# Prompt-phase attention mixer with a gated MLP: where half of each slot's fill work stands, who copies a fill bank, and the order of the last phase's first chunk

## The chip, the cores and the metric

The kernel runs on one core of one Trainium2 chip. The metric is device time in microseconds (us), the median of three runs. A core has a matrix engine (TensorE, PE in the profile, with its weight loads PEld beside it), VectorE (DVE), ScalarE (ACT), GpSimd (POOL), and SyncE (SP), on whose queue nearly all DMA transfers are issued. Matmul results land in PSUM banks, everything else in SBUF.

## The reference

One sequence of 2048 tokens with 512 features, all in float32. Attention has 32 heads of 16 features and looks back over a window of 256 keys; the MLP goes 512 to 1792 to 512. Cut to what matters:

```python
def layernorm(x):                       # no scale, no shift, eps 1e-5
    return (x - mean(x)) / sqrt(var(x) + eps)

def attention(x, wqkv, wo):             # H = 32, Dh = 16, W = 256
    q, k, v = split(x @ wqkv)
    scores = q @ k.T * Dh ** -0.5
    keep = (0 <= i - j) & (i - j < W)   # causal, sliding window
    p = softmax(where(keep, scores, -1e9))
    return merge_heads(p @ v) @ wo

def mlp(x, w1, b1, w2, b2):
    return gelu_tanh(layernorm(x) @ w1 + b1) @ w2 + b2

xn = layernorm(x)
out = x + attention(xn, wqkv, wo) * silu(mlp(xn, w1, b1, w2, b2))
```

## The kernel before, in words

**Number format.** Most matrix products are made with operands split in two: a high part rounded to TensorE's fp32r format and a low part that holds the rest. A product is then three matmuls (high with high, high with low, low with high; `PASSES`). Making such a pair is called splitting: one engine copies into the high part, another subtracts it from the raw value.

**Three phases.** A short prologue normalizes the first rows. Then a main loop (lines 620 to 642) runs t from -16 to 128; a value of t is called a slot here. Last come four chunks of 512 tokens for the MLP and the output (lines 693 to 783).

**What a slot holds.** Attention is done in 8 groups `n` of 4 heads, each over 16 key blocks of 128, so slots 0 to 127 are one block of one group each. On PE a slot issues, in this order:

1. `prob_block(..., 1)`: the scores of two of the four heads of this block into the only tile of its kind in PSUM, `stb`. ACT takes the exp of it into `pt` (SBUF), and POOL masks the triangles at its edges with `affine_select`. Those are the first scores below.
2. `max_block` for the block that is 12 slots ahead (`LEAD`): the same scores once more with queries as rows, into `xy` and `zo`; DVE merges them with a mask (`copy_predicated`) and takes each query's maximum. Every fourth slot `max_rows` transposes the maxima and sends them by DMA into the query rows, so that the scores come out with the maximum subtracted.
3. `fill_in(t, 0)` and `fill_in(t, 1)`: two helpings of other matmul work, called fills, out of the dictionary `fills`.
4. What `plan` has for this slot: copies, splits and DMAs set by `at(t, function, ...)`.
5. `prob_block(..., 0)`: the second scores, for the other two heads, into the same `stb`, with exp and masks.
6. `pv_step(t - 1)`: probabilities times V for the block before, four small matmuls for each of up to three key blocks, into `zo`; ACT copies the result to `oraw`, and every fourth slot a DMA sends it to `oT_d` in DRAM. V has a column of ones, so the sums of the softmax arrive as a row of the same result.

**The fills.** They are the Q/K projections of the next head groups (`pair_qk`, two pairs for each of the groups 1 to 7), the second half of the V projections (`pair_v`), six tiles of the MLP's hidden layer for the first chunk (`pair_h`, tiles f = 2 to 7, kept in DRAM as `h_d`), and the transposes of the MLP's input. `tandem(t0, t1, one, two)` lays two such jobs over the slots t0 to t1. It works with half matmuls: each step issues one with 64 rows on the upper half of the array and one on the lower half, into two PSUM banks `fb[0]` and `fb[1]`, first with one assignment of halves to banks, then with the other. At the first half of slot t1 both banks are complete and two `finish` functions follow. Each copies its bank out of PSUM. For Q/K, `finish` also sets `high` and `low` for slot t1 + 1 (even chunk) or t1 + 4 (odd chunk): a copy into the high part, a subtraction on POOL for the low part, and six sends by DMA from `sh` and `sl` into the rows of the slot buffer (`qk0` or `qk1`) of the group that is to come. `max_block` of that group reads these rows first.

**What sets the order.** The compute engines run their instructions in the order in which the program lists them (an `Ordered` wrapper keeps it); a scheduler may only place the instructions on SP's DMA queue, which then run one after the other. The pools matter too: raw loads, copies on their way, gelu results, sums, attention rows and residual rows all share five buffers of one pool, `t2`.

**The last phase.** A chunk has 14 tiles f of the hidden layer. Per tile: `hidden(f)`, 12 matmuls; `activate(f)`, gelu on ACT and a split into `gh` and `gl` on DVE; `project(f)`, 12 matmuls with the split W2 into the accumulators `accs`. Tiles are two deep: `hidden(f + 2)` stands behind `project(f - 1)`. In chunk 0 six of the tiles come out of `h_d` as `hr` instead, loaded three times two tiles by DMA. Chunk 0 also fetches and splits what W2 is still missing (`settle("w2", f)`, from `W2_FIRST`), loads Wo (`load_wo`), takes the reciprocal of all softmax sums at once (line 752, on a tile `den` of 128 x 512 loaded at f = 1) and sends it to `rden_d`. From f = 10, `load_o` fetches attention rows and reciprocals, and one step later `split_o` multiplies them on POOL and splits them on DVE into `ohl`. After the 14 tiles come silu, the Wo matmuls out of `ohl`, the product with the gate, the sum with x and the store. Input for the next chunk is loaded and normalized in between.

The main loop in its own words:

```python
prob_block(t // 16, t % 16, 1)
max_block(m // 16, m % 16)
fill_in(t, 0)
fill_in(t, 1)
for fn, args in plan.get(t, []):
    fn(*args)
prob_block(t // 16, t % 16, 0)
pv_step((t - 1) // 16, (t - 1) % 16)
```

Of the kernel before, what the change touches and what calls it, by code (L numbers as in the profile page):

```python
# [49 lines left out]
def mixer_kernel(ctx, tc, x, wqk, wv, wo, w1, b1, w2, b2, out):  # L50
# [245 lines left out]
    def pair_qk(n, c):  # L296
# [11 lines left out]
        def finish(ps, t):  # L308
# [3 lines left out]
            nc.scalar.copy(raw, ps)  # L312
# [17 lines left out]
    def pair_v(i):  # L330
# [7 lines left out]
        def finish(ps, t):  # L338
            nc.scalar.copy(vt[:, 2 * i: 2 * i + 2, :, 0:DH], ps.rearrange("p (b h d) -> p b h d", b=2, d=DH))
        return 6 * KT, mm, finish  # L340

    def pair_h(f):
# [5 lines left out]
        def finish(ps, t):  # L348
            raw = t2.tile([P, 512], F32, tag="t2", name=f"hr_{f}")
            nc.scalar.copy(raw, ps)  # L350
            nc.sync.dma_start(h_d[f - 2], raw)
        return 3 * KT, mm, finish

    def tandem(t0, t1, one, two, mid=None, back=None):
# [15 lines left out]
        fills[t1, 0].append((one[2], (fb[0], t1)))  # L370
        fills[t1, 0].append((two[2], (fb[1], t1)))
# [207 lines left out]
    for n, spans in enumerate((((-2, 2), (3, 8)), ((9, 15), (16, 23)), ((24, 31), (32, 39)), ((40, 46), (47, 51)),  # L579
                               ((56, 59), (68, 71)), ((76, 79), (80, 85)), ((86, 91), (92, 97))), 1):  # L580
        for c, (t0, t1) in zip((0, 2), spans):
            tandem(t0, t1, pair_qk(n, c), pair_qk(n, c + 1))
    for i, (t0, t1) in enumerate(((52, 55), (60, 63), (64, 67), (72, 75))):
        tandem(t0, t1, pair_v(2 * i), pair_v(2 * i + 1))
    for f, *at_ in ((2, 106, 112, None, None), (4, 113, 119, 115, None), (6, 120, 127, 123, 125)):
        tandem(*at_[:2], pair_h(f), pair_h(f + 1), *at_[2:])

    for n, t in enumerate((-7, 6, 21, 37, 53, 73, 83), 1):
# [6 lines left out]
    W2_FIRST = 4  # L595
    at(77, open_y)
    for i, t in enumerate((79, 81, 84, 87, 90, 92, 94, 96, 97, 98)):
        at(t, y_steps, i, i + 1)
    at(99, open_w1)
    for k, f in enumerate([*range(2, EARLY + 2), 0, 1, *range(EARLY + 2, NF)]):  # L600
        at(100 + 3 * k // 2, fetch, "w1", f)
        at(102 + 3 * k // 2, settle, "w1", f, k < 6)
    at(113, open_w2, 0)
    for f in range(W2_FIRST):
        at(115 + 3 * f, fetch, "w2", f)
        at(119 + 3 * f, settle, "w2", f)
    for kt in range(KT):
        (_, mm, _), = job_y(kt)[0]
        fills[101 + kt, 1] = [(mm, (0,))]
# [10 lines left out]
    for t in range(-16, end + 1):  # L620
# [13 lines left out]
        fill_in(t, 1)  # L634
        for fn, args in plan.get(t, []):
            fn(*args)
        if 0 <= t < end:
            prob_block(t // 16, t % 16, 0)
        if t >= 1:
# [33 lines left out]
    def fetch_sums():  # L673
        den = t2.tile([P, 512], F32, tag="t2", name="den")
        for g in range(4):
            nc.sync.dma_start(den[32 * g: 32 * g + 32], oT_d[g, :, DH].rearrange("a (c t) -> a c t", c=NCH))
        return den
# [15 lines left out]
    for c in range(NCH):  # L693
# [17 lines left out]

        def project(f):
# [104 lines left out]
```

## Time and profile before

| what | value |
|---|---|
| median of 3 runs | 842.91 us (840.06, 845.07, 842.91) |
| profiled execution, own time | 841.03 us |
| span of the profiled execution | 839.3 us |
| mean granted clock of TensorE | 0.983 |
| HBM read, written | 35.13 MB, 15.99 MB |

```profile
## 2 busy tenths in 40 slices
PE   5998788999989899898889889969999999999997
DVE  6875567877765555868774167342445335442233
ACT  5623567777665564776868622221112211131111
POOL 4002555756554454675755300121011201120013
PEclk9999899999999999999999989979999999999999
```

Each digit stands for a fortieth of the span, 21 us, and gives an engine's busy share in tenths. The loop with its slots fills the slices from the fourth to the twenty-third; the last phase is the rest, in which ACT, DVE and POOL have much less to do. The last row is the clock that TensorE was granted, in tenths of full speed. Span and the run's own time differ by what lies ahead of the first and behind the last instruction.

### The profile page before, as it was taken

How to read it: one execution, taken by the hardware profiler on the slowest of the kernel's cores; microseconds unless marked ns; L12 is line 12 of the kernel's file. 1: busy time of each engine (PE TensorE's matmuls, PEld its weight loads, DVE VectorE, ACT ScalarE, POOL GpSimd, SP SyncE). 2: the span in 40 equal slices, each digit the busy share in tenths (PEclk: the TensorE clock that was granted, in tenths of full speed). 3: DMA queues.
4: the chain of work that ended last, by engine and by line, in shares of the span. 5: the costliest groups of instructions: out<-in, count | busy, mean ns of one | idle time of the engine just before them, and what ended most of it. 6: DMA issues, size and time to landing. Idle time of an engine off the chain costs nothing. (4 is left out here: it accounts for less than half of the span.)

```text
span 839.3 us, 18438 instructions
## 1 busy us (share of the span) xinstructions
PE 760.6 (91%) x7384; PEld 594.0 (71%) x7384; DVE 467.6 (56%) x739; ACT 378.3 (45%) x643; POOL 288.3 (34%) x575
## 2 busy tenths in 40 slices
PE   5998788999989899898889889969999999999997
PEld 4876466666677777665666568748888888888886
DVE  6875567877765555868774167342445335442233
ACT  5623567777665564776868622221112211131111
POOL 4002555756554454675755300121011201120013
PEclk9999899999999999999999989979999999999999
DMA  8442345443453224446525353341013201310023
GB/s 278 149 92 54 91 96 143 103 106 84 118 116 84 68 55 128 96 112 155 138 73 160 102 186 93 107 127 38 12 38 101 101 0 38 92 72 1 26 69 107
DMA packets 51477, 79.98 MB, mean 95 GB/s; under 512 B 10112, under 2 KB 14208, under 8 KB 51392
## 3 DMA queue, kind: packets, MB, share of 16 engines
q1 hardware_dynamic: 51392, 78.80, 33.9%
q8 instruction: 58, 0.95, 0.5%
q14 instruction: 27, 0.22, 0.1%
HBM read 35.13 MB, written 15.99 MB: 61 GB/s over the span
## 5 line engine op out<-in xcount | busy, mean ns | idle before, releaser
L42 POOL TENSOR_SCALAR_AFFINE_SELECT pt<-pt 128x256 f32<-128x256 f32 x480 | 187.3, 414 | 204.8 <-ACT pt L42 202.2
L42 ACT ACTIVATE pt<-stb 128x768 f32<-128x768 f32 (+1 forms) x244 | 189.1, 775 | 112.4 <-PE stb L42 106.6
L42 DVE TENSOR_REDUCE mt<-xy 128x4 f32<-128x1024 f32 (+1 forms) x128 | 152.6, 1193 | 4.4
L42 PE MATMUL acc<-w,gh 128*128 128x512 f32 x448 | 141.5, 396 | 6.3 <-DVE gh L42 3.7
L42 DVE COPY_PREDICATED xy<-upper,zo 128x512 f32<-128x512 int32 x112 | 77.8, 695 | 104.5 <-PE zo L42 102.6
L42 PE MATMUL h<-yh,w1s 128*128 128x512 f32 x400 | 130.3, 389 | 0.4 <-ACT oraw L42 0.4
L42 PE MATMUL stb<-qk 64*128 64x384 f32 (+1 forms) x488 | 95.7, 386 | 35.9 <-ACT pt L42 26.6
L42 ACT ACTIVATE g<-h,b1s 128x512 f32<-128x512 f32 x50 | 34.5, 690 | 185.9 <-PE h L42 182.5
L42 PE MATMUL fb<-xnT,wqb 64*128 64x512 f32 (+1 forms) x720 | 112.7, 412 | 1.1 <-DVE xnT L42 1.1
L42 DVE CAST gh<-g 128x512 fp32r<-128x512 f32 x56 | 26.9, 480 | 152.1 <-PE acc L42 131.3
L42 PE MATMUL zo<-pt,vt 128*17 128x128 f32 x2880 | 104.8, 277 | 2.6 <-DVE xy L42 1.7
L42 PEld LDWEIGHTS acc<-w,gh 128*128 128x128 f32 x448 | 85.5, 191 | 26.6 <-DVE w L42 3.4
L42 PEld LDWEIGHTS stb<-qk 64*128 64x128 f32 x488 | 46.6, 185 | 81.0 <-ACT pt L42 75.1
L42 PEld LDWEIGHTS zo<-pt,vt 128*17 128x17 f32 x2880 | 68.2, 97 | 35.3 <-DVE xy L42 17.6
L42 PE MATMUL acc<-w,gl 128*128 128x512 f32 x224 | 88.5, 395 | 0.0
L42 PEld LDWEIGHTS h<-yh,w1s 128*128 128x128 f32 x400 | 75.1, 188 | 16.2 <-ACT oraw L42 0.7
L42 PE MATMUL h<-w1s 128*128 128x512 f32 x200 | 77.8, 389 | 0.0
L42 PEld LDWEIGHTS fb<-xnT,wqb 64*128 64x128 f32 (+1 forms) x720 | 69.9, 191 | 10.9 <-DVE xnT L42 1.5
L42 PE MATMUL xy<-qk 64*128 64x256 f32 (+2 forms) x536 | 61.9, 304 | 10.1 <-DMA qk<-sl 6.7
L42 POOL TENSOR_TENSOR or<-or,rec 128x512 f32<-128x512 f32 x16 | 21.1, 1318 | 143.6 <-DMA rec<-rden_d 127.5
L42 PEld LDWEIGHTS xy<-qk 64*128 64x128 f32 x536 | 45.3, 186 | 21.2 <-issue 9.1
L42 PE MATMUL s<-wos,ohl 128*128 128x512 f32 x192 | 47.3, 403 | 4.9 <-DVE ohl L42 4.9
(89 smaller groups left out, 848.2 us busy)
## 6 DMA issues: line engine op xcount, KB each, us to landing
qk<-sh SPq DMA_DIRECT2D x128, 128.0 KB
qk<-sl SPq DMA_DIRECT2D x64, 128.0 KB
oT_d<-oraw SPq DMA_DIRECT2D x32, 256.0 KB
x<-in_x_dram SPq DMA_DIRECT2D x16, 256.0 KB
or<-oT_d SPq DMA_DIRECT2D x16, 256.0 KB
rec<-rden_d SPq DMA_DIRECT2D x16, 256.0 KB
xo<-in_x_dram SPq DMA_DIRECT2D x16, 256.0 KB
out_dram<-xo SPq DMA_DIRECT2D x16, 256.0 KB
```

The lines of the kernel that those rows point to most:

```text
L42: r = issue(*args, **kwargs)
```

## The change

The diff does these things:

- In the loop, `fill_in(t, 1)` now stands behind the plan and the second scores, ahead of `pv_step`. `fill_in(t, 0)` stays.
- At the end of a pair, `fb[0]` is still copied by ACT, `fb[1]` by DVE.
- The first two Q/K projections of group 1 are no longer a tandem over slots -2 to 2 that ends with both copies in slot 2. They are two single jobs, spread over the half slots of -2 to 2, each of which sends its rows when it is done. The third and fourth are a tandem over slots 3 to 7 instead of 3 to 8.
- All other spans get new places: Q/K of groups 2 to 7 one to seven slots earlier, the V projections in 54 to 61 and 66 to 73, hidden tiles in 103 to 127 without slots between the pairs. The weights' fetches and splits, the steps that normalize the MLP's input, its transposes and the loads of W1 are set earlier with them.
- `W2_FIRST` goes from 4 to 7: seven W2 tiles are fetched and split in the loop, and `settle` in chunk 0 starts with the eighth, one at each step from the first on.
- `den` is loaded ahead of the chunks. The reciprocal comes in four parts of 128 columns at steps 4 to 7, and is sent at step 7.
- Chunk 0 takes the tiles in the order 2 to 7, 0, 1, 8 to 13, with `hidden(0)` and `hidden(1)` still issued first.
- `load_wo` stays at steps 8 to 11; `load_o` and `split_o` come two steps sooner in all chunks (8 to 11 and 9 to 12); in chunk 0 the loading and normalizing of the next chunk's input starts four steps later.

```diff
--- before.py
+++ after.py
@@ -305,11 +305,11 @@
         def send(src, qk, tt):
             copy_rows(slots[n % 2][tt:P:4, qk, :, sl], src[64 * qk: 64 * qk + 64])
 
-        def finish(ps, t):
+        def finish(ps, t, copy):
             hi = sgp.tile([P, 512], F32R, tag="sh", name=f"sh_{n}_{c}")
             lo = sgp.tile([P, 512], F32R, tag="sl", name=f"sl_{n}_{c}")
             raw = t2.tile([P, 512], F32, tag="t2", name=f"pjr_{n}_{c}")
-            nc.scalar.copy(raw, ps)
+            copy(raw, ps)
 
             def high():
                 nc.scalar.copy(hi, raw)
@@ -335,8 +335,8 @@
             nc.tensor.matmul(ps[:, 256 * j: 256 * (j + 1)], big[r, a, kt, P * kb: P * (kb + 1)], wva[r, b, kt],
                              **flags)
 
-        def finish(ps, t):
-            nc.scalar.copy(vt[:, 2 * i: 2 * i + 2, :, 0:DH], ps.rearrange("p (b h d) -> p b h d", b=2, d=DH))
+        def finish(ps, t, copy):
+            copy(vt[:, 2 * i: 2 * i + 2, :, 0:DH], ps.rearrange("p (b h d) -> p b h d", b=2, d=DH))
         return 6 * KT, mm, finish
 
     def pair_h(f):
@@ -345,9 +345,9 @@
             kt, (a, b) = k // 3, PASSES[k % 3]
             nc.tensor.matmul(ps, mlp["w1"][r, a, f, P * kt: P * (kt + 1)], mlp["yy"][b][kt][r], **flags)
 
-        def finish(ps, t):
+        def finish(ps, t, copy):
             raw = t2.tile([P, 512], F32, tag="t2", name=f"hr_{f}")
-            nc.scalar.copy(raw, ps)
+            copy(raw, ps)
             nc.sync.dma_start(h_d[f - 2], raw)
         return 3 * KT, mm, finish
 
@@ -367,8 +367,8 @@
                     (two if phase == 0 else one)[1](fb[1 - phase], i, hi, **flags)
                     (one if phase == 0 else two)[1](fb[phase], i, lo, **flags)
                 fills.setdefault(places[i * len(places) // n], []).append((unit, ()))
-        fills[t1, 0].append((one[2], (fb[0], t1)))
-        fills[t1, 0].append((two[2], (fb[1], t1)))
+        fills[t1, 0].append((one[2], (fb[0], t1, nc.scalar.copy)))
+        fills[t1, 0].append((two[2], (fb[1], t1, nc.vector.tensor_copy)))
 
     def spread(jobs, places):
 
@@ -576,37 +576,40 @@
     for t0, n, jobs in groups:
         fills.update(spread(jobs, [(t0 + i // 2, i % 2) for i in range(2 * n)]))
 
-    for n, spans in enumerate((((-2, 2), (3, 8)), ((9, 15), (16, 23)), ((24, 31), (32, 39)), ((40, 46), (47, 51)),
-                               ((56, 59), (68, 71)), ((76, 79), (80, 85)), ((86, 91), (92, 97))), 1):
+    for place, todo in spread([job_qk(1, 0), job_qk(1, 1)], [(t, k) for t in range(-2, 3) for k in range(2)]).items():
+        fills.setdefault(place, []).extend(todo)
+    tandem(3, 7, pair_qk(1, 2), pair_qk(1, 3), 6)
+    for n, spans in enumerate((((8, 13), (14, 20)), ((21, 28), (29, 36)), ((37, 42), (43, 48)), ((49, 53), (62, 65)),
+                               ((74, 77), (78, 82)), ((83, 88), (89, 94))), 2):
         for c, (t0, t1) in zip((0, 2), spans):
             tandem(t0, t1, pair_qk(n, c), pair_qk(n, c + 1))
-    for i, (t0, t1) in enumerate(((52, 55), (60, 63), (64, 67), (72, 75))):
-        tandem(t0, t1, pair_v(2 * i), pair_v(2 * i + 1))
-    for f, *at_ in ((2, 106, 112, None, None), (4, 113, 119, 115, None), (6, 120, 127, 123, 125)):
+    for i, (t0, t1) in enumerate(((54, 57), (58, 61), (66, 69), (70, 73))):
+        tandem(t0, t1, pair_v(2 * i), pair_v(2 * i + 1), 67 if t0 == 66 else None)
+    for f, *at_ in ((2, 103, 110, None, None), (4, 111, 118, 114, None), (6, 119, 127, 122, 123)):
         tandem(*at_[:2], pair_h(f), pair_h(f + 1), *at_[2:])
 
-    for n, t in enumerate((-7, 6, 21, 37, 53, 73, 83), 1):
+    for n, t in enumerate((-9, 6, 18, 34, 46, 70, 80), 1):
         at(t - 4, fetch_wqk, n)
         at(t, split_wqk, 0)
         at(t, split_wqk, 1)
     at(20, fetch_wv, 1)
     at(22, split_wv_part, 0)
     at(26, split_wv_part, 1)
-    W2_FIRST = 4
+    W2_FIRST = 7
     at(77, open_y)
-    for i, t in enumerate((79, 81, 84, 87, 90, 92, 94, 96, 97, 98)):
+    for i, t in enumerate((78, 79, 81, 83, 85, 87, 89, 91, 93, 94)):
         at(t, y_steps, i, i + 1)
-    at(99, open_w1)
+    at(95, open_w1)
     for k, f in enumerate([*range(2, EARLY + 2), 0, 1, *range(EARLY + 2, NF)]):
-        at(100 + 3 * k // 2, fetch, "w1", f)
-        at(102 + 3 * k // 2, settle, "w1", f, k < 6)
+        at(96 + 3 * k // 2, fetch, "w1", f)
+        at(98 + 3 * k // 2, settle, "w1", f, k < 6)
     at(113, open_w2, 0)
     for f in range(W2_FIRST):
-        at(115 + 3 * f, fetch, "w2", f)
-        at(119 + 3 * f, settle, "w2", f)
+        at(114 + 2 * f, fetch, "w2", f)
+        at(116 + 2 * f, settle, "w2", f)
     for kt in range(KT):
         (_, mm, _), = job_y(kt)[0]
-        fills[101 + kt, 1] = [(mm, (0,))]
+        fills[98 + kt, 1] = [(mm, (0,))]
 
     ln3 = layernorm(xs[3], "A3", True)
     lns = {-16: ln1[8:] + ln2[5:6], -14: ln2[6:8], -13: ln2[8:] + ln3[0:5], -12: ln3[5:8], -11: ln3[8:]}
@@ -631,11 +634,11 @@
         if 0 <= m < end:
             max_block(m // 16, m % 16)
         fill_in(t, 0)
-        fill_in(t, 1)
         for fn, args in plan.get(t, []):
             fn(*args)
         if 0 <= t < end:
             prob_block(t // 16, t % 16, 0)
+        fill_in(t, 1)
         if t >= 1:
             pv_step((t - 1) // 16, (t - 1) % 16)
         run(lns.get(t, ()))
@@ -670,11 +673,9 @@
         raw = load(t2, "t2", wo[:, 512 * g: 512 * (g + 1)], f"wor{g}")
         split(wos[:, 0, g], wos[:, 1, g], raw)
 
-    def fetch_sums():
-        den = t2.tile([P, 512], F32, tag="t2", name="den")
-        for g in range(4):
-            nc.sync.dma_start(den[32 * g: 32 * g + 32], oT_d[g, :, DH].rearrange("a (c t) -> a c t", c=NCH))
-        return den
+    den = t2.tile([P, 512], F32, tag="t2", name="den")
+    for g in range(4):
+        nc.sync.dma_start(den[32 * g: 32 * g + 32], oT_d[g, :, DH].rearrange("a (c t) -> a c t", c=NCH))
 
     def load_o(c, g):
 
@@ -709,52 +710,53 @@
             split(gh, gl, g, nc.vector.tensor_copy)
             gs[f] = (gh, gl)
 
+        order = [*made, *(f for f in range(NF) if f not in made)]
+
         def project(f):
             gh, gl = gs.pop(f)
             for i in range(4):
                 acc = accs[i // 2][:, i % 2]
                 sl = slice(P * i, P * (i + 1))
                 for k, (a, b) in enumerate(((gh, 0), (gh, 1), (gl, 0))):
-                    nc.tensor.matmul(acc, a[:, sl], w2_part(b, f), start=(f == 0 and k == 0),
-                                     stop=(f == NF - 1 and k == 2))
+                    nc.tensor.matmul(acc, a[:, sl], w2_part(b, f), start=(f == order[0] and k == 0),
+                                     stop=(f == order[-1] and k == 2))
 
         hidden(0)
         hidden(1)
-        for f in range(NF + 1):
-            if f < NF:
-                activate(f)
-            if c == 0 and f < NF:
-                if f >= W2_FIRST:
-                    settle("w2", f)
-                    if f + 2 < NF:
-                        fetch("w2", f + 2)
-                if f >= 8 and f < 12:
-                    load_wo(f - 8)
-            if f >= 1:
-                project(f - 1)
-            if f + 2 < NF and f + 2 not in made:
-                hidden(f + 2)
+        late = 4 if c == 0 else 0
+        for i in range(NF + 1):
+            if i < NF:
+                activate(order[i])
+            if c == 0 and W2_FIRST + i < NF:
+                settle("w2", W2_FIRST + i)
+                if W2_FIRST + i + 2 < NF:
+                    fetch("w2", W2_FIRST + i + 2)
+            if i >= 1:
+                project(order[i - 1])
+            if i + 2 < NF and order[i + 2] not in made and order[i + 2] > 1:
+                hidden(order[i + 2])
+            if c == 0 and 4 <= i < 8:
+                nc.vector.reciprocal(den[:, P * (i - 4): P * (i - 3)], den[:, P * (i - 4): P * (i - 3)])
+                if i == 7:
+                    nc.sync.dma_start(rden_d.rearrange("g a (c t) -> (g a c) t", c=NCH), den)
+            if c == 0 and 8 <= i < 12:
+                load_wo(i - 8)
             if c + 1 < NCH:
-                if f == 2:
+                if i == 2 + late:
                     mlp["y"] = load_x(c + 1, ((mlp["yp"], "y"),), "y")
                     mlp["ln"] = layernorm(mlp["y"], f"C{c + 1}_0", False)
-                elif f == 7:
+                elif i == 7 + late:
                     mlp["ln"] = layernorm(mlp["y"], f"C{c + 1}_1", False)
-                if f in (4, 7):
+                if i - late in (4, 7):
                     y_steps(0, 2)
-                elif f in (5, 8):
+                elif i - late in (5, 8):
                     y_steps(2, 5)
-                elif f in (6, 9):
+                elif i - late in (6, 9):
                     y_steps(5, 10)
-            if c == 0 and f == 1:
-                den = fetch_sums()
-            if c == 0 and f == 4:
-                nc.vector.reciprocal(den, den)
-                nc.sync.dma_start(rden_d.rearrange("g a (c t) -> (g a c) t", c=NCH), den)
-            if 11 <= f < 15:
-                os_.append(split_o(c, f - 11, *wanted))
-            if 10 <= f < 14:
-                wanted = load_o(c, f - 10)
+            if 9 <= i < 13:
+                os_.append(split_o(c, i - 9, *wanted))
+            if 8 <= i < 12:
+                wanted = load_o(c, i - 8)
         us = [accs[i // 2][:, i % 2] for i in range(4)]
         for u in us:
             nc.vector.tensor_add(u, u, b2s)
```

## The prediction, made before the changed kernel had run

> **What bounds the kernel now.** I read the page, busy time by stretch, the waits, the timeline of two slots, then the last phase by itself.
>
> ```profile
> span 839.3 us, 18438 instructions
> PE 760.6 (91%) x7384; PEld 594.0 (71%) x7384; DVE 467.6 (56%) x739; ACT 378.3 (45%) x643; POOL 288.3 (34%) x575
> L42 ACT COPY oraw<-zo 128x128 f32<-128x128 f32 x128 | 34.6, 271 | 5.1 <-PE zo L42 4.9
> ```
>
> TensorE (PE) is the engine to save on. Each slot ends with one copy of the PV result (`oraw`, 128 of them); I used these as slot marks and cut the loop at them (15, 33, 31, 19, 16 and 13 slots), and the last phase at its first two chunks. Columns: length, busy time and instructions of each engine, granted clock, DMA.
>
> ```profile
> 78.50:132.10 53.60, 43.00 (x634) 30.96 (x634) 32.64 (x43) 32.68 (x58) 27.44 (x61) 0.94 0.37 92
> 132.10:227.50 95.40, 87.69 (x1328) 62.22 (x1328) 71.55 (x95) 68.64 (x121) 59.67 (x133) 1.00 0.46 109
> 227.50:339.60 112.10, 100.54 (x1618) 80.17 (x1618) 65.30 (x91) 67.63 (x120) 54.01 (x124) 0.98 0.36 87
> 339.60:396.90 57.30, 51.23 (x764) 36.73 (x764) 43.97 (x63) 40.32 (x71) 36.98 (x80) 1.00 0.52 125
> 396.90:447.30 50.40, 43.25 (x646) 30.75 (x646) 38.21 (x53) 36.54 (x67) 31.57 (x67) 1.00 0.43 123
> 447.30:474.00 26.70, 24.60 (x418) 16.43 (x418) 7.09 (x12) 25.12 (x51) 17.58 (x46) 1.00 0.41 123
> 474.00:569.00 95.00, 80.99 (x328) 63.92 (x329) 48.74 (x88) 25.27 (x39) 11.09 (x9) 0.91 0.41 125
> 569.00:658.00 89.00, 89.00 (x402) 73.78 (x402) 38.52 (x74) 15.16 (x23) 12.59 (x10) 1.00 0.18 60
> ```
>
> The first stretch takes 3.57 us a slot, the second 2.89, the dense third 3.62, the next two 3.02 and 3.15. In chunk 1 of the last phase (569 to 658) PE never rests; chunk 0 is longer, although six of its fourteen hidden tiles were made in the loop. In the loop PE waits for almost one thing, scores behind the exp that empties `stb`:
>
> ```profile
> PEld stb L42 <- ACT pt L42: 75.1, 141, 1.7
> ```
>
> The end of a fill pair, and the slot after it:
>
> ```profile
> 303.21 1.14 PE L42 MATMUL fb<-xnT,wqb 64*128 64x512 f32 x8
> ...
> 304.18 0.33 PE L42 MATMUL stb<-qk 64*128 64x384 f32 x2
> ...
> 304.38 1.07 ACT L42 COPY pjr<-fb 128x512 f32<-128x512 f32 x2 [0.49 <-PE fb L42]
> ...
> 305.34 0.83 ACT L42 ACTIVATE pt<-stb 128x768 f32<-128x768 f32 x1
> ...
> 306.22 0.19 PEld L42 LDWEIGHTS stb<-qk 64*128 64x128 f32 x2 [1.20 <-ACT pt L42]
> ...
> 306.79 0.81 ACT L42 ACTIVATE pt<-stb 128x768 f32<-128x768 f32 x1 [0.46 <-PE stb L42]
> ...
> 307.05 1.68 PE L42 MATMUL fb<-wva,xnT 64*128 64x256 f32 x24
> ...
> 308.54 0.37 PE L42 MATMUL stb<-qk 64*128 64x384 f32 x2
> ...
> 308.83 0.85 PE L42 MATMUL zo<-pt,vt 128*17 128x128 f32 x24
> 308.94 0.81 ACT L42 ACTIVATE pt<-stb 128x768 f32<-128x768 f32 x1 [0.84 <-PE stb L42]
> ...
> 309.80 0.19 PEld L42 LDWEIGHTS stb<-qk 64*128 64x128 f32 x2 [0.40 <-ACT pt L42]
> ...
> 310.49 1.64 PE L42 MATMUL fb<-wva,xnT 64*128 64x256 f32 x24
> ```
>
> First scores at 306.22, their exp from 306.79 for 0.81, so the second scores cannot follow before 1.43. All fills lie between them: 1.49 for 12 V pairs (307.05 to 308.54, 0.124 each); a QK pair takes 0.24 (303.21 to 304.18, four). From second to next first scores the exp makes it 1.26, though PE has only 0.29 + 0.85 = 1.14 to do. With f the fill time and 0.69 for scores and maxima (309.80 to 310.49), a slot takes max(1.43, 0.69 + f) + 1.26.
>
> **Fills on both sides of the second scores.** A slot becomes max(c, 0.69 + f/2) + max(c, 1.14 + f/2), c being 1.26 where PE arrives running and 1.43 where it arrives stalled. Dense slots (f = 1.4): 3.35 before, 1.39 + 1.84 = 3.23 after. I take 0.12 for 31 dense slots and 0.1 for the 13 after them: 5 us. The bounds are nothing (if the exp, not PE, sets both gaps) and 0.31 a dense slot, 10 in all, if the 0.19 weight load hides too. At f = 0.72 it was 2.69 and is between 2.7 and 2.86: +0.1 in 20 slots, +2. What is queued behind the moved fills on PE is PV and the next first scores; the built order shows them so.
>
> **One copy on DVE.** Both copies of a pair stood on ACT ahead of the second exp (304.38 to 305.34), and the next scores waited 1.20 instead of 0.40.
>
> ```profile
> L42 ACT COPY pjr<-fb 128x512 f32<-128x512 f32 x32 | 17.4, 589 | 16.9 <-PE fb L42 14.7 <-PE stb L42 2.0
> L42 DVE TENSOR_TENSOR w1s<-fb,yh 128x512 fp32r<-128x512 f32 x4 | 2.7, 679 | 0.0
> ```
>
> ACT loses one copy, 1.07 - 0.59 = 0.48 at each of the 13 pair ends from slot 49 on, 6 us; in sparser slots the spare exp time took it. The bounds: 0, and 0.80 at all 21 ends, 17. DVE's copy, not in the trace, I bound by 0.59 and 0.68 (its own read of `fb`). Behind it on DVE stands the next slot's mask and maximum; DVE is busy 65.30 of 112.10 us in the dense stretch, 1.5 us idle a slot, so I cost it at nothing. Without that cover it is 21 x 0.68 = 14.
>
> **Slot 1's projections made sooner.** The first two go alone into slots -2 to 2, their copies and sends by half slots.
>
> ```profile
> 86.81 1.20 SPq L42 DMA_DIRECT2D qk<-sl  x2
> ...
> 89.95 0.69 PE L42 MATMUL xy<-qk 64*128 64x128 f32 x4 [4.20 <-DMA qk<-sl]
> ```
>
> Maxima of head group 1 waited 4.20 us for rows sent at 86.81, about 3 us before they landed; the first chunk is now ready two slots (5.8 us) earlier, the second two, the third one. The fifteen slots at the second stretch's 2.89 make 43.4; some 1 us goes to the fills pulled in: 53.6 - 44.5 = 9. Bounds 4 (the one wait) and 10.
>
> **Tail of the loop.** ACT sets it (25.12 of 26.70 busy): three more W2 tiles there, three hidden copies fewer, at 0.6 each: nothing. Hidden and W1 work moved up by three or four slots: 3.15 towards 3.02 in 16 slots, 2.
>
> Loop: 9 + 5 + 6 + 2 - 2 = 20.
>
> **Chunk 0.** At chunk 1's 0.221 a matmul (89.00 / 402) it would be 89.0 - 72 x 0.221 = 73.1; 21.9 is lost, nearly all here:
>
> ```profile
> 479.60:487.10 7.50, 5.64 (x17) 4.07 (x17) 3.27 (x6) 2.04 (x4) 0.00 (x0) 0.77 0.69 236
> 497.00:504.60 7.60, 5.11 (x15) 3.51 (x14) 7.29 (x14) 2.36 (x4) 1.12 (x1) 0.78 0.26 75
> 537.00:545.80 8.80, 6.83 (x27) 4.56 (x26) 4.43 (x8) 2.91 (x4) 1.86 (x2) 1.00 0.32 108
> 546.50:569.10 22.60, 14.94 (x60) 11.69 (x59) 9.40 (x15) 5.50 (x9) 5.11 (x5) 0.77 0.43 128
> ```
>
> By the same price they lose 3.7, 4.3, 2.8 and 9.3.
>
> ```profile
> 473.70 0.27 ACT L42 COPY oraw<-zo 128x128 f32<-128x128 f32 x1 [0.46 <-PE zo L42]
> ...
> 477.11 1.28 ACT L42 ACT_TABLE_LOAD   x1 [3.14 <-PE h L42]
> 478.41 0.69 ACT L42 ACTIVATE g<-h,b1s 128x512 f32<-128x512 f32 x1
> ...
> 480.98 1.41 SPq L42 DMA_DIRECT2D hr<-h_d  x3
> ...
> 484.79 1.34 ACT L42 ACTIVATE g<-hr,b1s 128x512 f32<-128x512 f32 x2 [4.31 <-DMA hr<-h_d]
> ...
> 495.28 3.35 DVE L42 RECIPROCAL den<-den 128x512 f32<-128x512 f32 x1
> ```
> ```profile
> 553.25 0.43 DVE L42 CAST ohl<-or 128x512 fp32r<-128x512 f32 x1 [5.56 <-POOL or L42]
> ```
>
> Early tiles first costs: the first gelu now waits for `hr`, landed at 484.79, 10.8 after the last `oraw` (473.97); in the built order the table load waits with it. 10.8 + 1.3 + 0.7 + 0.5 (a DVE step, 48.74 / 88) = 13.3, while PE's two hidden tiles end at 24 x 0.23 = 5.6: 7.7 idle instead of some 2, +5.7. In front of `hr` on SP stand two `den` loads; it waited anyway. The reciprocal leaves the path: quarters of 0.84 beside three DVE steps of 0.55 are 2.5, under the 12 x 0.22 = 2.7 of a projection: 4.3 back. Without that cover, up to 3.35 again. W2 is settled by tile 6 and attention rows are split two tiles sooner, two tiles being up to 10.9 of PE time: the last two losses, 12.1, fall to 1.5. Net 4.3 + 10.6 - 5.7 = 9 to 11; I take 11, since fewer stalls also mean less half clock. Bounds 0 and 16 (`hr` early).
>
> At 0.69 the gelu starts 0.02 after its table load. The Trainium skill, "ScalarE: Activation LUTs", What ACT_TABLE_LOAD costs, adds a drain of 1.38 us, which would make the sum 1.4 longer; the row shows none. Both the 479.6 and the 497 stretches, with about 2 us idle each, ran at clock 0.77. The Trainium skill, "TensorE: Matmul & The Clock Gate", Part 1, has half clock after an idle window of some 3.4 us, so the new idle alone would pay about 1.7 more; the row has before paying already, so I add none.
>
> **The sum.** 839.3 - 20 - 11 = 808.3 of span; 841.03 - 839.3 = 1.7 lies around it: 810.0. The profiled run is 1.9 under the median of 842.91; on the median 31 less is 812, and I say 811.
>
> **Rivals.**
> - Chunk 0 gains nothing: `hr` at 13.3 and late attention rows eat it. For: both are DMA chains on one SP queue. Against: the rows leave SP two tiles earlier. 822.
> - DVE's copies show: +14, 825. Against: DVE's idle time.
> - Slower: the fills behind the second scores delay PV and next scores by their full length while the gap ahead stays at the exp's 1.43. Half of all fills (14 x 24 + 3 x 24 QK-sized pairs of 0.24, 4 x 48 of 0.124: 122 us) is 61: 811 + 61 = 872; it decides from half that exposure on. For: sparse slots do this. Against: 1.14 of work stands in a gap of 1.26.
> - Faster: weight loads hide in every dense slot, and `hr` comes early: 811 - 5 - 5 - 6 = 795.
> - The change does not do what it says: 842; the built order speaks against it.
>
> **How the numbers follow.** Forecast 0.66 (its own range 801 to 821), chunk 0 nothing 0.14, DVE 0.06, slower 0.06, faster still 0.06, no effect 0.02. The 8-in-10 range reaches to the next two cases, 799 to 828. Within 0.5%, 4.2 us, is about what a measurement of this kernel can tell from no change: faster 0.92, same 0.02, slower 0.06.
>
> **What would show it.** Right: no 4 us wait of `xy` for `qk<-sl`; the sum of `stb` waiting for `pt` well under 75.1; stretches one to five shorter by 9, 0, 8, 2 and 2; chunk 0 near 84 with a longer hole before its first projection and none around the reciprocal. Wrong: dense slots still at 3.6, or scores of chunk 0 still waiting for `ohl`.

## The result and the profile after

The changed kernel takes 811.38 us (median of 4, 810.2 to 816.42) against 843.99 us before: ratio 0.9632, 95% interval 0.9577 to 0.9686. The profiled execution took 810.2 us, its span is 808.5. In some executions of nearly every kernel here TensorE's clock is halved for a while in the loop, which spreads the times of one kernel by several us; parts of the change are therefore compared by the length of their stretch, and a granted clock under 1.00 in it is told beside it.

Busy time in the page after, and from its waits the one that stood at 75.1 us:

```profile
PE 758.0 (94%) x7360; PEld 583.3 (72%) x7360; DVE 483.7 (60%) x762; ACT 371.1 (46%) x623; POOL 289.7 (36%) x575
```
```profile
PEld stb L42 <- ACT pt L42: 55.5, 131, 1.3
```

PE works as long as before (758.0 against 760.6), in a span that is 30.8 us shorter. The busy time by stretch, cut at the same slots (columns as before):

```profile
77.45:122.90 45.45, 44.44 (x652) 30.67 (x650) 33.04 (x45) 30.87 (x54) 27.99 (x62) 1.00 0.46 108
122.90:218.60 95.70, 92.11 (x1342) 61.31 (x1338) 75.09 (x100) 69.66 (x120) 60.71 (x133) 1.00 0.45 114
218.60:321.50 102.90, 98.40 (x1621) 79.37 (x1620) 71.14 (x99) 62.72 (x108) 53.05 (x125) 1.00 0.36 95
321.50:378.80 57.30, 51.98 (x752) 34.81 (x748) 46.58 (x65) 40.96 (x72) 39.19 (x81) 1.00 0.51 131
378.80:425.50 46.70, 43.49 (x638) 28.30 (x636) 38.93 (x55) 35.32 (x61) 30.65 (x67) 1.00 0.42 119
425.50:452.50 27.00, 24.65 (x420) 15.78 (x418) 8.72 (x14) 24.61 (x48) 16.86 (x45) 1.00 0.41 122
452.50:538.60 86.10, 75.82 (x329) 61.72 (x330) 49.20 (x89) 22.49 (x36) 11.12 (x9) 0.94 0.42 132
538.60:627.40 88.80, 88.80 (x401) 73.70 (x400) 38.99 (x74) 16.43 (x24) 12.27 (x10) 1.00 0.18 60
```

Against the rows of before the stretches changed by -8.2, +0.3, -9.2, 0, -3.7, +0.3, -8.9 and -0.2. With 1.1 less ahead of the first cut and 0.2 less behind the last these are the 30.8. The marks of before lie up to 0.3 beside the ends of the copies; from end to end in both, the front gives 1.3, the last slots of the loop cost 0.6 and chunk 0 gives 9.2, and the rest stays.

Before had a low clock in the first stretch (0.94) and in the third (0.98), which the changed kernel doesn't have in the profiled execution. In the third it is these 4 us, worth 1.7 of full clock:

```profile
323.00:327.00 4.00, 4.00 (x44) 2.71 (x42) 1.57 (x2) 1.13 (x3) 1.33 (x4) 0.58 0.83 233
```

A dense slot in the timeline after:

```profile
247.42 0.44 PE L42 MATMUL stb<-qk 64*128 64x384 f32 x2
...
248.15 0.93 PE L42 MATMUL fb<-wva,xnT 64*128 64x256 f32 x12
...
248.92 0.38 PE L42 MATMUL stb<-qk 64*128 64x384 f32 x2
...
249.13 0.87 PE L42 MATMUL fb<-wva,xnT 64*128 64x256 f32 x12
...
250.72 0.44 PE L42 MATMUL stb<-qk 64*128 64x384 f32 x2
```

Six V pairs stand on each side of the second scores (248.92), and PE runs through: 3.30 from first scores to first scores. The slot with the same 12 pairs, before, took 3.58 (306.22 to 309.80). The prediction's formula has 3.32 for it now: 1.44 to the second scores and 1.88 from there, with fills of 1.49; measured are 1.50 and 1.80.

The start of chunk 0, from the timelines of ACT, SP and PE:

```profile
464.10 1.28 ACT L42 ACT_TABLE_LOAD   x1 [11.59 <-DMA hr<-h_d]
465.39 0.72 ACT L42 ACTIVATE g<-hr,b1s 128x512 f32<-128x512 f32 x1
```
```profile
452.53 0.52 SPq L42 DMA_DIRECT2D oT_d<-oraw  x1
...
460.15 1.42 SPq L42 DMA_DIRECT2D hr<-h_d  x3
```
```profile
466.62 1.22 PE L42 MATMUL acc<-w,gh 128*128 128x512 f32 x2 [8.31 <-DVE gh L42]
```

The predicted longer hole is there: 8.31 us before the first projection, since ACT waits 11.59 for `hr`, and SP issues `hr` only at 460.15, 7.6 after the last attention block's store was issued, and 0.07 after that store landed (460.08 by its semaphores); SP's wait for this store is 4.8. The buffers of `hr` lie where the loop's were.

What PE waited for in chunk 0, before and then after:

```profile
PE s L42 <- DVE ohl L42: 4.9, 1, 4.9
PE acc L42 <- DVE gh L42: 3.7, 3, 1.9
PE yt L42 <- DVE w1s L42: 2.7, 1, 2.7
PE acc L42 <- DVE w L42: 2.5, 3, 0.8
```
```profile
PE acc L42 <- DVE gh L42: 10.2, 2, 8.3
```

The waits for `ohl`, `w1s` and `w`, 10.1 together, are gone, and those for `gh` are 6.5 longer. By the rows PE idles 10.3 instead of 14.0; the other 5.2 of the 8.9 are busy time (75.8 instead of 81.0 for the same matmuls), at a clock of 0.94 instead of 0.91.

### The profile page after: what moved, and what is told of

The parts are those of the page before. It is cut to its first block, busy times and chain, and to the rows that moved or that the text cites. A ratio compares the mean times of both kernels' runs of the same rounds, so it can differ in the third digit from the quotient of the medians.

```text
span 808.5 us, 18389 instructions
## 1 busy us (share of the span) xinstructions
PE 758.0 (94%) x7360; PEld 583.3 (72%) x7360; DVE 483.7 (60%) x762; ACT 371.1 (46%) x623; POOL 289.7 (36%) x575
## 4 chain that ended last, share of the span: by engine, by line
PE 73%; issue 9%; ACT 8%; DVE 4%; DMA 2%; POOL 1%; SPq 1%; POOLq 0%; ACTq 0%; DVEq 0%
PE acc L42 14%; PE fb L42 14%; PE h L42 14%; PE zo L42 11%; PE stb L42 9%; ACT pt L42 6%; PE s L42 4%; PE xy L42 4%; PE pv L42 2%; DVE mt L42 1%; DVE xnT L42 1%; DVE xy L42 1%; SPq L42 1%; DMA x<-in_x_dram 1%; DMA rec<-rden_d 1%
## 5 line engine op out<-in xcount | busy, mean ns | idle before, releaser
L42 POOL TENSOR_SCALAR_AFFINE_SELECT pt<-pt 128x256 f32<-128x256 f32 x480 | 189.4, 418 | 186.4 <-ACT pt L42 184.1
L42 PE MATMUL acc<-w,gh 128*128 128x512 f32 x448 | 139.7, 393 | 10.2 <-DVE gh L42 10.2
L42 DVE COPY_PREDICATED xy<-upper,zo 128x512 f32<-128x512 int32 x112 | 77.8, 694 | 78.2 <-PE zo L42 75.1
L42 PE MATMUL fb<-xnT,wqb 64*128 64x512 f32 (+1 forms) x696 | 118.9, 405 | 1.7 <-DVE xnT L42 1.7
L42 DVE CAST gh<-g 128x512 fp32r<-128x512 f32 x56 | 28.9, 516 | 146.3 <-PE acc L42 118.3
L42 PE MATMUL stb<-qk 64*128 64x384 f32 (+1 forms) x488 | 100.2, 407 | 16.5 <-ACT pt L42 13.8
L42 PEld LDWEIGHTS h<-yh,w1s 128*128 128x128 f32 x400 | 75.1, 188 | 16.3 <-ACT oraw L42 0.7
L42 PEld LDWEIGHTS fb<-xnT,wqb 64*128 64x128 f32 (+1 forms) x696 | 64.7, 186 | 7.9 <-DVE xnT L42 2.1
L42 POOL TENSOR_TENSOR rsC<-veC,mhalf 128x4 f32<-128x4 f32 x7 | 7.1, 1011 | 143.0 <-DVE veC L42 143.0
L42 ACT COPY oraw<-zo 128x128 f32<-128x128 f32 x128 | 34.2, 267 | 47.4 <-PE zo L42 45.4
```

The costliest lines, as they stand in the source:

```text
L42: r = issue(*args, **kwargs)
```

## The experiments

Each is the changed kernel with the edit shown. What each costs is read from its stretches against those of the changed kernel: 45.47, 95.65, 102.97, 57.26, 46.66, 27.05 and, for chunk 0, 86.06, now cut exactly at the ends of the attention copies. One execution of each run was profiled. In stretches that an edit leaves alone, at full clock, these lengths repeat within 0.1 in slots 1 to 15 and 49 to 79, but slots 16 to 48 are anywhere from 95.6 to 96.8, and chunk 0, with its own clock of 0.94 to 0.96, from 84.4 to 86.6 where its code is untouched. Less than that says nothing.

| run | median, range | ratio to before (95%) | against the changed kernel, us by stretch |
|---|---|---|---|
| e1_fills_ahead | 813.8, 812.74 to 817.16 | 0.9670 (0.9644 to 0.9695) | slots 49 to 79 +2.9, 16 to 48 0.0, 80 to 98 +1.5 (clock 0.98) |
| e2_both_copies_act | 818.13, 815.86 to 821.39 | 0.9713 (0.9687 to 0.9739) | first five stretches +0.8, +1.4, +3.2, +0.1, +0.8 |
| e3_first_pair_tandem | 821.89, 816.08 to 822.94 | 0.9738 (0.9708 to 0.9767) | slots 1 to 15 +7.5 (clock 0.94) |
| e4_tiles_0_1_first | 808.0, 804.57 to 812.65 | 0.9598 (0.9568 to 0.9628) | chunk 0 -6.2 |
| e5_whole_reciprocal | 811.17, 809.3 to 813.73 | 0.9627 (0.9601 to 0.9653) | chunk 0 +0.2 |
| e6_rows_two_steps_later | 819.15, 816.07 to 823.51 | 0.9725 (0.9692 to 0.9759) | chunk 0 +5.1, chunk 1 +0.4 |
| e7_both_copies_dve | 820.09, 816.44 to 821.62 | 0.9729 (0.9699 to 0.9758) | first three stretches +0.6, +2.3, +1.6 |
| e8_last_span_to_97 | 811.67, 810.21 to 813.42 | 0.9627 (0.9602 to 0.9652) | slots 80 to 98 -0.2 |
| e9_next_input_not_delayed | 813.84, 809.7 to 821.47 | 0.9657 (0.9616 to 0.9699) | chunk 0 -0.7 |
| e10_four_w2_tiles | 813.37, 808.8 to 818.77 | 0.9652 (0.9613 to 0.9691) | chunk 0 -0.1 |
| n1_tiles_kept | 809.93, 806.4 to 815.96 | 0.9615 (0.9579 to 0.9651) | chunk 0 -3.5 |
| n2_last_pair_kept | 805.9, 801.92 to 808.65 | 0.9547 (0.9509 to 0.9584) | chunk 0 -6.2 |

**Fills ahead of the second scores again.**

```diff
         fill_in(t, 0)
+        fill_in(t, 1)
         for fn, args in plan.get(t, []):
...
             prob_block(t // 16, t % 16, 0)
-        fill_in(t, 1)
```

> The changed kernel with one part undone: the second helping of fills stands ahead of the plan and the second scores again. By the prediction's step (5 us from dense slots, 2 given back by sparse ones) this costs about 3 us, 814, with slots 49 to 79 longer by about 4 and slots 16 to 48 shorter by about 2. A rival that gives the whole gain of the dense slots to this move expects 9 or more, 820; one that gives it to the single copy on DVE and the new spans expects nothing, 811.

Measured, slots 16 to 48 and 49 to 79 of this run:

```profile
124.30:220.00 95.70, 88.90 (x1338) 63.11 (x1338) 76.53 (x100) 69.11 (x120) 61.73 (x135) 1.00 0.46 114
220.00:325.90 105.90, 98.71 (x1620) 79.41 (x1622) 70.31 (x99) 62.51 (x109) 52.08 (x123) 1.00 0.35 92
```

The dense slots lose 2.9 of their 9.2, and PE's weight loads for `stb` wait 16.7 for `pt` there instead of 8.8; the sparse ones are as long as with the move. So it is one part of several, and the price on sparse slots isn't there.

**Both copies on ACT, both on DVE.**

```diff
-        fills[t1, 0].append((two[2], (fb[1], t1, nc.vector.tensor_copy)))
+        fills[t1, 0].append((two[2], (fb[1], t1, nc.scalar.copy)))
```
```diff
-        fills[t1, 0].append((one[2], (fb[0], t1, nc.scalar.copy)))
+        fills[t1, 0].append((one[2], (fb[0], t1, nc.vector.tensor_copy)))
```

> The changed kernel with both banks of a pair copied by ACT again. By the prediction's step ACT has 0.48 us more ahead of an exp at 13 pair ends: 6 us longer, 817, nearly all of it in slots 49 to 79. A rival, that the fills behind the second scores now cover the copies, expects nothing, 811; the upper bound of the prediction, 0.80 at all 21 ends, would give 828.

> The changed kernel with both banks of a pair copied by DVE. The prediction costs a DVE copy at nothing, since DVE idles 1.5 us a slot: then ACT is freed of one more copy ahead of an exp, and the time is the same or up to 6 us less, 805 to 811. Its rival, that DVE's copies stand in front of the next mask and maximum, expects 0.68 at each of 21 ends more: 825.

Measured, slots 49 to 79 with both on ACT, then with both on DVE:

```profile
220.20:326.40 106.20, 98.43 (x1624) 79.40 (x1620) 66.77 (x92) 65.95 (x115) 53.30 (x125) 1.00 0.35 92
```
```profile
221.10:325.60 104.50, 99.64 (x1620) 79.80 (x1620) 74.47 (x106) 60.01 (x101) 52.30 (x123) 1.00 0.35 93
```

Both on ACT cost 6.3, but only half of it in the dense slots, where the matmuls of `stb` wait 7.7 for `pt` instead of 4.3. Slots 1 to 15 pay 0.8 too; the 1.4 in slots 16 to 48 is little more than the 1.1 by which these differ anyway.

Both on DVE cost 4.5 in the first three stretches, although ACT is freed further: there PE's waits of `stb` for `pt` fall from 7.2 to 3.8. In their place stands a wait that the changed kernel doesn't have:

```profile
PE fb L42 <- DVE pjr L42: 3.7, 9, 0.5
PE fb L42 <- DVE vt L42: 1.5, 4, 0.4
```

The next pair's fills wait 5.2 for a bank that DVE hasn't emptied yet. The weight loads that wait for DVE's mask (`zo` for `xy`) lose no more than in the changed kernel: 5.9 against 6.3 in these stretches. So the second copy in a row comes too late for the bank; that copies delay the mask, as the rival had it, doesn't show.

**The first pair as a tandem.**

```diff
-    for place, todo in spread([job_qk(1, 0), job_qk(1, 1)], [(t, k) for t in range(-2, 3) for k in range(2)]).items():
-        fills.setdefault(place, []).extend(todo)
+    tandem(-2, 2, pair_qk(1, 0), pair_qk(1, 1))
...
+        if t < 3:
+            fill_in(t, 1)
...
-        fill_in(t, 1)
+        if t >= 3:
+            fill_in(t, 1)
```

> The changed kernel with the first two projections of head group 1 as a tandem over slots -2 to 2 again; so that this can be ordered, the second helping of fills stands in its old place for t below 3. By the prediction's step the rows come too late for the maxima again, and the later chunks behind them: 8 us longer in slots 1 to 15, 819. A rival, that only the single wait of 4.20 us was worth anything, expects 815; another, that the projections' place is not what made the wait, expects 811.

Measured, slots 1 to 15 and the wait in them:

```profile
78.82:131.75 52.93, 46.59 (x656) 32.91 (x658) 34.83 (x46) 31.29 (x55) 28.77 (x63) 0.94 0.42 99
```
```profile
PE xy L42 <- DMA qk<-sl: 4.1, 1, 4.1
```

The wait of 4.1 is back, the clock in the stretch falls from 1.00 to 0.94, and the stretch is 7.5 longer: the size of the first theory, but hardly by its second half, the later chunks. Behind the wait the clock is low:

```profile
88.00:96.00 8.00, 6.54 (x54) 4.70 (x54) 2.63 (x4) 1.98 (x4) 1.47 (x4) 0.57 0.16 33
```

These 8.00 us at 0.57 are worth up to 3.4 of full clock; with the wait that can be the whole 7.5. The edit also puts the fills of the slots below 3 back ahead of the second scores, which wasn't tried by itself.

**The order of the tiles in chunk 0.**

```diff
-        order = [*made, *(f for f in range(NF) if f not in made)]
+        order = [*range(NF)]
```

> The changed kernel with chunk 0's tiles in the order 0 to 13 again. The hole of 8.31 us ahead of the first projection is by the prediction the price of the early tiles first (5.7): without it 805, with the first projection starting near 461. A rival, that the order is what lets W2, the reciprocal and the attention rows come in time, expects the hole to move elsewhere: 811 or more.

Chunk 0 takes 79.90 instead of 86.06, with a hole of 2.45 ahead of the first projection, which starts 8.2 after the last attention copy instead of 14.1. The hole did not move elsewhere: PE waits 3.9 for `gh` in the whole chunk, instead of 10.2. The tile order, one of the change's own parts, is a loss of 6.2; without it the median is 3.4 lower, with intervals that overlap.

**The whole reciprocal, the next input's old place, four W2 tiles.**

```diff
             if c == 0 and 4 <= i < 8:
-                nc.vector.reciprocal(den[:, P * (i - 4): P * (i - 3)], den[:, P * (i - 4): P * (i - 3)])
+                if i == 4:
+                    nc.vector.reciprocal(den, den)
```
```diff
-        late = 4 if c == 0 else 0
+        late = 0
```
```diff
-    W2_FIRST = 7
+    W2_FIRST = 4
```

> The changed kernel with the reciprocal in one piece at step 4 again, sent at step 7 as now. By the prediction's step the parts give back 4.3 us, so the whole costs 4 more, 815, as a wait of the projection behind it for gh. A rival, that the parts only spread the same DVE time and the tiles from DRAM leave no room for either, expects nothing, 811.

> The changed kernel with the next chunk's input loaded and normalized at its old steps in chunk 0 (2 to 9 instead of 6 to 13), the reciprocal still in four parts. The whole reciprocal cost nothing when it was put back; if the cause is that the statistics no longer stand beside it on DVE, they cost 2 to 4 us in chunk 0 when they come back: 813 to 815. If the early tiles or the W2 tiles are the cause, nothing changes: 811.

> The changed kernel with four W2 tiles fetched and split in the loop instead of seven; chunk 0 then settles the other ten, one at each step from the first on, until step 9. Late attention rows alone gave back 5 us where the prediction had 10.6 for them and W2 together. If W2 in the loop has the other half, chunk 0 is 5 us longer with waits for ohl: 816, less up to 2 in the last slots of the loop. If not, the rest came from the delayed input: 809 to 811.

None of the three shows a cost in chunk 0: +0.2, -0.7 and -0.1, inside the 2.2 by which it differs anyway. The third undoes only the number of W2 tiles split in the loop: chunk 0 still splits one at each step from the first on, three or more steps ahead of its use, where before split a tile one step ahead. That lead was not undone in any run.

DVE's timeline gives a reason for the reciprocal, with the whole one put back, and then before:

```profile
478.74 0.43 DVE L42 CAST gh<-g 128x512 fp32r<-128x512 f32 x1 [0.90 <-PE acc L42]
...
480.48 3.35 DVE L42 RECIPROCAL den<-den 128x512 f32<-128x512 f32 x1
483.74 0.36 DVE L42 CAST gh<-g 128x512 fp32r<-128x512 f32 x1
```
```profile
491.85 0.43 DVE L42 CAST gh<-g 128x512 fp32r<-128x512 f32 x1 [1.50 <-PE acc L42]
...
498.55 0.36 DVE L42 CAST gh<-g 128x512 fp32r<-128x512 f32 x1
```
```profile
499.06 0.47 PE L42 MATMUL acc<-w,gh 128*128 128x512 f32 x1 [1.66 <-DVE gh L42]
```

From one `gh` to the next it is 5.00 us now and 6.70 before. PE has two tiles to project meanwhile (`gh` has two buffers), 24 x 0.221 = 5.3. So 3.35 alone fits, and 3.35 with the 1.7 of statistics for the next chunk's input (493.59 to 495.28) doesn't: 1.4 over, where PE rested 1.66 before. By this reckoning parts or the later input are each enough, and undoing one shows nothing. Both undone at once weren't tried, so it stays an argument.

**The attention rows two steps later.**

```diff
-            if 9 <= i < 13:
-                os_.append(split_o(c, i - 9, *wanted))
-            if 8 <= i < 12:
-                wanted = load_o(c, i - 8)
+            if 11 <= i < 15:
+                os_.append(split_o(c, i - 11, *wanted))
+            if 10 <= i < 14:
+                wanted = load_o(c, i - 10)
```

> The changed kernel with the attention rows loaded and split two steps later again, in all chunks. By the prediction's step the first scores against Wo in chunk 0 wait for ohl again: 10.6 us, 822, with the wait of about 9 us ahead of the matmuls into s. A rival, that the seven W2 tiles settled in the loop and the earlier reciprocal have made room in the five shared buffers anyway, expects 811 to 813.

Chunk 0 is 5.1 longer, but the scores wait for `ohl` only 0.47. The larger wait is another, in the timelines of PE and DVE:

```profile
534.62 1.97 PE L42 MATMUL yt<-ident,y 128*128 128x128 f32 x8 [3.16 <-DVE w1s L42]
```
```profile
530.81 2.76 DVE L42 TENSOR_TENSOR acc<-acc,b2s 128x512 f32<-128x512 f32 x4
533.87 1.29 DVE L42 TENSOR_TENSOR w1s<-yt,yh 128x512 fp32r<-128x512 f32 x2 [0.30 <-ACT yh L42]
```

The last late split (530.20, 0.69) holds up the four sums on DVE behind it, those the split of the next input's transposes, and PE waits 3.16 for that. Behind it the granted clock is low again, 0.74 from 534 to 545. The early rows have a price, too: the changed kernel rests 1.85 at 520.7, since a `gh` stands on DVE behind a split of `ohl` that waits 2.37 for POOL, and with late rows that rest is not there.

**The hole at the start of chunk 0, twice.** First tiles 2 and 3 were kept, then tiles 6 and 7, each with the last attention block copied into the same buffer; the second also has the longer Q/K span of the next experiment.

```diff
+            if f < 4:
+                mlp["kept"][f] = mlp["gated"][:, f]
+                copy(mlp["kept"][f], ps)
+                return
...
-            outs[0] = sgp.tile([P, 512], F32, tag="or", name=f"oraw_{n}_{qb}", bufs=2)
+            outs[0] = (mlp["gated"][:, 0] if n == NQ - 1 and qb == 12 else
+                       sgp.tile([P, 512], F32, tag="or", name=f"oraw_{n}_{qb}", bufs=2))
...
-        order = [*made, *(f for f in range(NF) if f not in made)]
+        order = [2, 3, 0, 1, *range(4, NF)] if made else [*range(NF)]
```
```diff
+            if f >= 6:
+                mlp["kept"][f] = mlp["gated"][:, f - 4]
...
-    for f in range(0, EARLY, 2):
+    for f in range(0, EARLY - 2, 2):
...
-        order = [*made, *(f for f in range(NF) if f not in made)]
+        order = [6, 7, 0, 1, *range(2, 6), *range(8, NF)] if made else [*range(NF)]
```

> The changed kernel, with hidden tiles 2 and 3 kept in the buffer of the gate instead of going through DRAM, the last attention block copied into the same buffer so that nothing of the last phase has to wait for its transfer, and the tiles of chunk 0 in the order 2, 3, 0, 1, 4 and so on. By the theory that the 8.31 us hole is the wait for hr behind that transfer, the first projection starts behind the second hidden tile, near 458 instead of 466.6: 8.3 less, and the clock that was halved behind the hole some 2 more, 801. A rival, that the hole has a second cause (W2, the bias, a buffer of the last phase), expects 805 to 811.

> The changed kernel with the last hidden pair, tiles 6 and 7, kept in the gate's buffer instead of going through DRAM (tiles 2 to 5, stored ten and more slots before the end, still go that way), the last attention block copied into the same buffer, chunk 0 in the order 6, 7, 0, 1, 2 to 5, 8 to 13, and the last Q/K tandem drawn out to slot 97. When tiles 2 and 3 were kept, the first gelu waited for the store of tiles 6 and 7, issued late; now no transfer issued at the end of the loop stands in front of it. The theory that the hole of 8.3 us is these transfers alone expects the first projection right behind the second hidden tile, 5.8 us after the last attention copy, chunk 0 near 76 us, and 800 to 802 with a clock of 0.99. A rival, that the store was only the last of several waits (shared buffers, the order of the queue), expects half of it: 805 to 807.

ACT's timeline of the first, then of the second:

```profile
470.04 1.28 ACT L42 ACT_TABLE_LOAD   x1 [7.98 <-DMA h_d<-hr]
```
```profile
453.57 1.28 ACT L42 ACT_TABLE_LOAD   x1
454.86 0.72 ACT L42 ACTIVATE g<-gated,b1s 128x512 f32<-128x512 f32 x1
...
469.40 0.62 ACT L42 CAST w<-w2r 128x512 fp32r<-128x512 f32 x1 [9.76 <-DMA w2r<-in_w_dram]
```

In the first the gelu waits for the store of tiles 6 and 7 instead (hole 4.78). In the second the gelu starts 0.01 after its table load, and the first projection follows the second hidden tile at once. But now the split of a W2 tile, in front of the fourth gelu on ACT's queue, waits 9.76 for its load, and PE rests 3.63 at 467.5. About half of the hole is gained, as the rival said: chunk 0 79.8, and 805.9 in all, the lowest median of these kernels. But tiles 0 and 1 first gave 79.9 with nothing kept, so keeping the pair shows no gain over that order.

**The clock.**

```diff
-                               ((74, 77), (78, 82)), ((83, 88), (89, 94))), 2):
+                               ((74, 77), (78, 82)), ((83, 88), (89, 97))), 2):
```

> The changed kernel, with only the last Q/K tandem drawn out from slots 89 to 94 to slots 89 to 97, so that the slots 94 to 97 have fills again. In several executions of the kernels so far the clock is halved for 8 to 30 us from slot 94 on, where TensorE rested for more than 1 us. If that rest sets it off, no execution has it there any more: clock 0.99 in all, the median near the best times of the changed kernel, 809 to 810, and a narrower spread. If it comes at random, the spread stays 810 to 817.

Measured, from slot 94 on:

```profile
364.00:366.00 2.00, 1.77 (x38) 1.21 (x34) 1.63 (x2) 0.38 (x1) 0.80 (x2) 1.00 0.24 34
366.00:396.00 30.00, 26.95 (x370) 17.65 (x370) 23.72 (x35) 24.73 (x43) 23.28 (x46) 0.94 0.53 150
```

TensorE is busy 1.77 of the 2.00 us in which it had 0.97 (last section). The range shrinks to 3.2 us, the clock is 0.988 to 0.994 in all six executions, and a short half clock is left (0.94 over the 30 us). The median is no lower than the changed kernel's, so the 809 to 810 that were expected did not come; why isn't shown.

## Why the prediction was right

The forecast was 811 and a span of 808.3; measured were 811.38 and 808.5. By its steps:

- **Loop, -20.** The stretches sum to -20.5, with 1.1 more ahead of them. Forecast were -9, 0, -8, -2 and -2, measured -8.2, +0.3, -9.2, 0 and -3.7; the tail, at nothing, gave +0.3 (+0.6 from end to end).
- **Slot 1's projections, -9.** Put back, they cost 7.5, between the bounds of 4 and 10: 4.1 of wait, and up to 3.4 for the low clock behind it, which the prediction didn't name. Before, too, had 0.94 in this stretch.
- **Fills on both sides, -5 and +2.** Undone, +2.9 in the dense slots and 0.0 in slots 16 to 48; the +1.5 in slots 80 to 98 came at a clock of 0.98 and can't be told from that. The sum of 3 holds, but as 2.9 and nothing: 5 was too much, and the 2 for sparse slots did not show.
- **One copy on DVE, -6.** Undone, +6.3. The size was right and the place was not quite: 3.2 in slots 49 to 79, and 0.8 in slots 1 to 15, where "in sparser slots the spare exp time took it". These two steps make 6.1 of the 9.2 in slots 49 to 79. Another 1.7 is the low clock that only before had there. The last 1.4, to which the new places of the spans are left, wasn't tried by itself.
- **Early tiles first, +5.7.** Undone, -6.2. The trace has the wait for `hr` as worked out: table load at 11.6 after the last copy (10.8 forecast), 8.31 idle (7.7).
- **The reciprocal, -4.3.** This step failed as an account of cause: the whole reciprocal costs 0.2, where 4.3 would stand clear of the 2.2 by which chunk 0 differs. What before paid was, by the reckoning above, reciprocal and statistics together, 6.70 against 5.3 of cover, and the prediction had only the first.
- **The last two losses, -10.6.** Of them 5.1 are the attention rows. The wait that came back was not the predicted one for `ohl` but the one behind it on DVE (3.16; before had 2.7 of it). The number of W2 tiles split in the loop shows nothing; the lead of the splits in chunk 0 wasn't undone. The waits themselves are gone (10.1, in the result), but which edit removed the rest, or whether several do it together, stays open.
- **The clock.** The terms for chunk 0 sum to 9.2, and 8.9 to 9.2 were measured. The prediction took 11, since fewer stalls should mean less half clock; these 1.8 did not come. Behind the new hole the granted clock is 0.78 over 10 us (466.6 to 476.6), 2.2 of full clock; before had 0.77 in its stretch of 7.5. By the Trainium skill, "TensorE: Matmul & The Clock Gate", Part 1, the prediction had an estimate of 1.7 for the new idle, and left it out. The 2.2 is near it, though before shows the low clock after a rest of 1.9 as well.
- **The table load.** The Trainium skill, "ScalarE: Activation LUTs", What ACT_TABLE_LOAD costs, adds a drain of 1.38 us; the rows after again have none: load at 464.10 for 1.28, gelu at 465.39.

So the loop came out by the steps that were named, with some sizes off. That the total is within 1 us is partly luck: chunk 0 gained 9 instead of 11, the loop and its front 1.5 more than 20, and in chunk 0 the sum of the terms is better confirmed than the terms. Of the rivals, the slower one fell at once: PE runs through the dense slots, as the gap of 1.26 with 1.14 of work said. The DVE rival didn't come for one copy, and for two the cost is at the bank and not at the mask.

## What to carry to other kernels

When an engine's queue has a slow instruction, count what stands between two deliveries to the bottleneck and hold it against the bottleneck's buffered work: 5.0 against 5.3 cost nothing that shows, 6.7 went with a rest of 1.66. Cutting the slow one or moving its neighbour may then be the same cure. Work made early pays only if its way back is short: follow the buffers that the phases share, for a store of the old phase can stand in front of a load of the new one. Undoing each part of a change by itself finds the part that is a loss (here 6 us) inside a change that is a gain. It can't price two parts that cover for each other; for those both have to be undone at once.

## What the runs showed of the hardware

The same rest of TensorE of about a microsecond (1.03, for `xy`) was followed by 30 us of half clock in one execution and by none in another. From slot 94 on, by stretch, with tiles 0 and 1 first (whose loop is that of the changed kernel), and the changed kernel itself:

```profile
364.00:366.00 2.00, 0.97 (x28) 0.83 (x29) 1.97 (x4) 0.94 (x3) 1.68 (x3) 1.00 0.51 138
366.00:396.00 30.00, 27.27 (x254) 17.92 (x245) 17.58 (x25) 18.18 (x31) 16.80 (x35) 0.52 0.49 139
```
```profile
364.00:366.00 2.00, 0.97 (x19) 0.83 (x23) 1.97 (x4) 1.16 (x3) 1.46 (x2) 1.00 0.48 128
366.00:396.00 30.00, 25.68 (x386) 16.72 (x375) 23.98 (x34) 23.98 (x41) 22.80 (x47) 1.00 0.57 161
```

The same 0.97 of work in 2.00 us goes before a clock of 0.52 for 30 us, in which 254 matmuls run instead of 386, and before a full clock. From the second half of slot 94 through slot 97 there are no fills. Of the 40 executions with that loop (four of the changed kernel, six each of e4, e5, e6, e9, e10 and n1) 19 have a mean clock under 0.988. With fills drawn out to slot 97 (e8 and n2) none of 12 has; their lowest is 0.988. This mean takes in chunk 0, whose code differs among these runs, so the count makes it likely that the rest sets the half clock off, and no more. The Trainium skill, "TensorE: Matmul & The Clock Gate", Part 1, has half clock after an idle window of some 3.4 us and full clock again after some 3.4 us of sustained work, with a window that runs freely. The chance would fit such a window; a rest of 1.03 is shorter than it, and PE was 91% busy (27.27 of 30.00) through the 30 us at half clock.
